# Loads of token mixtures ordered behind the copies of dense sums, one load for each copy

## The chip, the cores and the metric

One core of one Trainium2 chip runs the whole kernel. The metric is the device time of one execution in microseconds (us). The core has a matrix engine (TensorE, PE in the profile), a vector engine (VectorE, DVE), an engine for activations (ScalarE, ACT), a general engine (GpSimd, POOL), and an engine that here only issues transfers (SyncE, SP). All of them take their instructions in order, each from a queue of its own, and meet through semaphores.

## The reference

For 2048 tokens x of width 512 (float32), with 32 heads of width 16 and a hidden width of 1792:

```
g   = sigmoid(sum(x * gate_w))                         # one gate per token
q, k, v = split(x @ wqkv)                              # 32 heads of 16
a   = concat_heads(softmax(q k^T / 4) v) @ wo
b   = (sigmoid(x @ w_gate) * (x @ w_up)) @ w_down
out = g * a + (1 - g) * b
```

## The kernel before

Scores are the main work: for each of the 16 pairs of heads the kernel makes the 2048 x 2048 scores of both heads twice. Once, keys by queries, they go through the exponential into the product with the values (`st_part`, line 646, and `values`, line 787). Once before that, queries by keys, they only give each query's maximum (`sm_step`, lines 300 and 302). The maxima are transposed by VectorE into tiles `mt` (line 324), and four small transfers (line 330) put them as two extra rows into the tile `qs` that holds the queries of the pair. There are two `qs` tiles, used by alternate pairs. So `st_part` can begin on a block of 512 queries only when the maxima of this block have landed in `qs`. One block of one pair takes four steps of the main loop; in each step TensorE works on both heads of the pair, on a piece of "dense" work, and ends with the 32 matmuls of `values`.

The dense work is taken from the generator `filling` and spread over the steps, 24 half matmuls to one sum. A sum is one 128x512 tile in the PSUM bank `dn`, and takes two steps. First come 24 sums of the projections of q and k (line 154 is the matmul). After the last matmul of a sum ScalarE copies `dn` into SBUF: this is the function `leave` (line 578). GpSimd then splits the copy into a high and a low part (lines 255 and 252), and SP stores both to DRAM, to `q_d` or to `k_d` (line 254). After these 24 sums come those of the gate and up projections. They do not multiply by x itself but by "token mixtures", sums and differences of blocks of x (the table `MIX`), that the kernel makes itself while the first 24 sums run:

- `mixing(pair)` makes them in 16 pieces for one half of the tokens, one piece for each dense sum: a load of parts of x into an SBUF buffer (line 341; two buffers in turn), an addition on GpSimd (line 346), a cast and a subtraction (362, 350), and a store of 512 KB to DRAM, to `xm_d` (line 351). A load into a buffer waits until the store of the piece before last, which used it, has been written.
- `mixed(pair, j)` makes four loads from `xm_d` into one SBUF tile, `xm`, 512 KB each (line 371), and puts them on the list `parts`. The buffer is one that held x for the projections, and is free when the sums with that part of x are done.
- `take(n, behind)` issues the next n loads of this list. With `behind` it adds a dependency: the load waits for that instruction.

For the first half of the tokens the lists are filled after sums 12, 16, 22 and 24, and one load is taken after each sum up to the 20th, two after each later one. The call, inside `filling`, is

```
left = leave(e.bitcast(F32), run.o)
...
take(2 if runs > 21 else 1, left if runs < 21 else None)
```

What sets the order: on TensorE, ScalarE, VectorE and GpSimd the instructions stand in the order in which the program is written (`ORDERED`). SP is not among these; where its transfers stand is decided by the framework's scheduler, by what each one waits for. Nearly all of the kernel's transfers are issued on SP's queue, and every one of this document is. SP issues them in order, so that one that waits holds all behind it.

The functions that the change touches, and what calls them:

Of the kernel before, what the change touches and what calls it, by code (L numbers as in the profile page):

```python
# [52 lines left out]
def gated_mix(ctx, tc, x, xc, xmix, wqk, wv, wo, w_gu, w_down, gate_w, out):  # L53
# [439 lines left out]
    def filling():  # L493
# [19 lines left out]
        for j, (n, cp) in enumerate(jobs):  # L513
            settle([raw for raw, _, _ in coming])
            ws, nxt = nxt, []
            for c in range(2):
                for i, w in enumerate(ws):
                    run = Sum(bankd(), unit(w, 2 * cp + c))
                    yield run
                    runs += 1  # L520
                    e = keep.tile([P, 512], F32R, name=f"qk{n}_{cp}_{c}_{i}", tag="er", bufs=6)
                    left = leave(e.bitcast(F32), run.o)
                    put_qk(e, (q_d, k_d)[i], n, 2 * cp + c)
                    next(mix, None)
                    if j + 1 < len(jobs):
                        if (c, i) == (0, 0):
                            coming = raws(jobs[j + 1][0])
                        elif (c, i) != (1, 1):
                            nxt.append(split_weights(coming[len(nxt)]))
                    elif (c, i) != (0, 0):  # L530
                        weights()
                    if runs in (12, 16, 22, 24):
                        T[len(T)] = mixed(0, len(T))
                    take(2 if runs > 21 else 1, left if runs < 21 else None)
# [4 lines left out]
        for cp in range(2):  # L539
            for fp in range(NF // 2):  # L540
                for a in range(2):
                    arrive = combine(cp, fp, a)
                    order = [(j, g) for j in range(3) for g in ((LOW, UP) if a else (UP, LOW))] + [(3, LOW if a else UP)]
                    ws = []
                    for q, (j, g) in enumerate(order):
                        if len(ws) <= j:
                            ws.append(W.pop(0))
                        run = Side(bankd(), g, ws[j], T[j])
                        yield run
                        m = ((2, 1), (4, 3), (7, 6), (5, 5))[j][g]  # L550
                        e = keep.tile([P, 512], F32, name=f"m{m}_{cp}_{fp}_{a}", tag="er", bufs=6)
                        leave(e, run.o)
                        if arrived:
                            arrived.pop(0)()
                        arrived.append(lambda arrive=arrive, m=m, e=e: arrive(m, e))
                        if q in (0, 2, 3, 4, 6):
                            weights()
                        if t % 4 == 1:
                            next(mix, None)
                        t += 1  # L560
                        if cp == 0 and fp == NF // 2 - 1 and a == 1 and q in (2, 4, 6):
                            late_t[q // 2 - 1] = mixed(1, q // 2 - 1)
                        take(1 if late_t and q < 4 and not cp else 2)
                        if cp and fp == NF // 2 - 1 and a:
                            if q == 1:
                                load_ahead()
                            elif q > 1:
                                weights_ahead()
# [6 lines left out]
    exps, lately = [], [None]  # L575

    def leave(e, o):
        lately[0] = act.activation(e, o, AF.Copy)  # L578

    fill = filling()  # L580

# [486 lines left out]
```

## Time and profile before

| | |
|---|---|
| Time before, median of 3 runs | 1666.73 us (1665.47 to 1667.89) |
| Time of the profiled execution | 1666.75 us |
| Its span, from the first to the last instruction | 1664.9 us |
| Mean granted TensorE clock | 0.997 |
| TensorE matmuls busy | 1651.4 us, 99% of the span |
| VectorE, ScalarE, GpSimd busy | 86%, 80%, 63% |
| Transfers on SP's queue | 233.37 MB, 47.1% of 16 DMA engines |

Rows of a timeline give the start in us from the start of the span, the duration, the engine, the line of the code, the operation, what it writes and reads ("out<-in"), and how many such instructions stand together. "SPq" is SP's queue: its rows are the issues of transfers, not the transfers. In brackets stands the idle time of the engine just before, and what ended it. A row of windows gives the start and end of a stretch, its length, the busy time of each engine with the number of its instructions, the mean granted TensorE clock (1.00 is full speed), the mean busy share of the 16 DMA engines and their GB/s. A row of waits gives who waited for whom: the sum in us, how often, the longest.

### The profile page before, as it was taken

How to read it: one execution, taken by the hardware profiler on the slowest of the kernel's cores; microseconds unless marked ns; L12 is line 12 of the kernel's file. 1: busy time of each engine (PE TensorE's matmuls, PEld its weight loads, DVE VectorE, ACT ScalarE, POOL GpSimd, SP SyncE). 2: the span in 40 equal slices, each digit the busy share in tenths (PEclk: the TensorE clock that was granted, in tenths of full speed). 3: DMA queues.
4: the chain of work that ended last, by engine and by line, in shares of the span. 5: the costliest groups of instructions: out<-in, count | busy, mean ns of one | idle time of the engine just before them, and what ended most of it. 6: DMA issues, size and time to landing. Idle time of an engine off the chain costs nothing.

```text
span 1664.9 us, 44107 instructions
## 1 busy us (share of the span) xinstructions
PE 1651.4 (99%) x16842; PEld 1180.0 (71%) x16842; DVE 1427.0 (86%) x2456; ACT 1334.3 (80%) x2928; POOL 1051.8 (63%) x1238
## 2 busy tenths in 40 slices
PE   9999989999999999999999999999999999999999
PEld 7866756666666666766766766766776776678887
DVE  6989979999999999999999999999999999667643
ACT  4188868889889888888888999999999988974321
POOL 1146654457888888767666897877777767753110
PEclk9999989999999999999999999999999999999999
DMA  9624675364444434442347453424343425269850
GB/s 260 133 81 163 192 224 162 104 180 128 139 149 128 147 121 138 123 129 78 96 131 194 146 143 116 114 97 100 99 103 95 111 84 179 80 231 298 297 172 26
DMA packets 131555, 236.71 MB, mean 142 GB/s; under 512 B 19408, under 2 KB 39888, under 8 KB 128336
## 3 DMA queue, kind: packets, MB, share of 16 engines
q1 hardware_dynamic: 131056, 233.37, 47.1%
q8 instruction: 133, 2.18, 0.6%
q14 instruction: 78, 0.64, 0.2%
q10 hardware_dynamic: 288, 0.52, 0.1%
HBM read 155.71 MB, written 77.59 MB: 140 GB/s over the span
## 4 chain that ended last, share of the span: by engine, by line
PE 98%; DVE 1%; DMA 1%; POOL 0%; SPq 0%; ACT 0%; issue 0%; POOLq 0%; DVEq 0%
PE dn L174 26%; PE sm L787 17%; PE st L787 12%; PE dn L154 7%; PE sm L300 6%; PE sm L646 6%; PE sm L1004 6%; PE st L646 4%; PE st L141 4%; PE st L300 4%; PE dn L1004 2%; PE st L154 1%; PE st L1004 1%; DVE stat L302 1%; DMA xm_d<-xm 0%; PE st L89 0%
## 5 line engine op out<-in xcount | busy, mean ns | idle before, releaser
L302 DVE TENSOR_REDUCE stat<-sm 128x1 f32<-128x512 f32 x1199 | 763.2, 681 | 77.9 <-PE st L646 52.5
L648 ACT ACTIVATE p<-sm 128x512 f32<-128x512 f32 (+1 forms) x1314 | 668.4, 593 | 15.4 <-PE sm L646 14.1
L302 DVE TENSOR_REDUCE stat<-st 128x1 f32<-128x512 f32 x849 | 549.7, 681 | 46.7 <-PE sm L646 45.2
L648 ACT ACTIVATE p<-st 128x512 f32<-128x512 f32 (+2 forms) x982 | 515.6, 594 | 1.2 <-PE st L646 0.5
L174 PE MATMUL dn<-xm,mh 64*128 64x512 f32 x1568 | 484.6, 389 | 0.0
L646 PE MATMUL sm<-qs,ks 64*128 64x512 f32 (+1 forms) x1314 | 472.8, 383 | 7.8 <-DMA qs<-mt 7.8
L300 PE MATMUL sm<-ks,qs 48*128 48x512 f32 x1199 | 476.7, 420 | 0.1
L646 PE MATMUL st<-qs,ks 64*128 64x512 f32 (+2 forms) x982 | 362.9, 382 | 0.7 <-DVE v L627 0.7
L300 PE MATMUL st<-ks,qs 48*128 48x512 f32 x849 | 357.7, 422 | 0.0
L174 PE MATMUL dn<-xm,ml 64*128 64x512 f32 x784 | 303.9, 388 | 0.0
L174 PEld LDWEIGHTS dn<-xm,mh 64*128 64x128 f32 x1568 | 289.7, 185 | 14.6
L646 PEld LDWEIGHTS sm<-qs,ks 64*128 64x128 f32 x1314 | 235.1, 187 | 70.9 <-DVE stat L302 59.2
L787 PE MATMUL sm<-p,v 128*17 128x256 f32 x4672 | 280.6, 381 | 0.0
L300 PEld LDWEIGHTS sm<-ks,qs 48*128 48x128 f32 x1199 | 210.8, 184 | 33.3 <-ACT p L648 26.7
L787 PEld LDWEIGHTS sm<-p,v 128*17 128x17 f32 x4672 | 122.9, 97 | 130.3 <-ACT p L648 44.7
L646 PEld LDWEIGHTS st<-qs,ks 64*128 64x128 f32 x982 | 177.8, 187 | 48.0 <-DVE stat L302 44.9
L787 PE MATMUL st<-p,v 128*17 128x256 f32 x3520 | 211.4, 381 | 0.1
L813 POOL TENSOR_TENSOR sum<-sum,part 128x256 f32<-128x256 f32 x192 | 141.5, 737 | 66.7 <-ACT part L792 29.6
L425 POOL TENSOR_TENSOR m<-m,m 128x512 f32<-128x512 f32 x140 | 178.1, 1290 | 4.2 <-ACT m L578 2.1
L300 PEld LDWEIGHTS st<-ks,qs 48*128 48x128 f32 x849 | 157.3, 185 | 22.7 <-ACT p L648 20.1
L787 PEld LDWEIGHTS st<-p,v 128*17 128x17 f32 x3520 | 92.7, 97 | 98.2 <-ACT p L648 33.5
L174 PEld LDWEIGHTS dn<-xm,ml 64*128 64x128 f32 x784 | 144.3, 184 | 9.9
(314 smaller groups left out, 2342.8 us busy)
## 6 DMA issues: line engine op xcount, KB each, us to landing
r<-in_w_gu_dram SPq DMA_DIRECT2D x112, 256.0 KB
gul<-gu_d SPq DMA_DIRECT2D x56, 512.0 KB
gu_d<-m SPq DMA_DIRECT2D x84, 256.0 KB
xm_d<-xm SPq DMA_DIRECT2D x32, 512.0 KB
xm<-xm_d SPq DMA_DIRECT2D x32, 512.0 KB
xm<-in_xmix_dram SPq DMA_DIRECT2D x24, 512.0 KB
qs<-q_d SPq DMA_DIRECT2D x90, 128.0 KB
ks<-k_d SPq DMA_DIRECT2D x90, 128.0 KB
```

Source lines behind the costliest of these rows:

```text
L141: pe.matmul(o, a, b, start=(i == 0), stop=(i == len(ops) - 1))
L154: mm = pe.matmul(self.o, a[rows], b[rows], start=(self.n == 0), stop=(self.n == 2 * len(self.ops) - 1))
L174: pe.matmul(self.o, a, b, start=(self.n == 0), stop=(self.n == len(self.ops) - 1))
L300: pe.matmul(t, qs[r:r + KM, qt * P:(qt + 1) * P], ks[r:r + KM, g * 512:(g + 1) * 512], start=True, stop=True)
L302: dve.tensor_reduce(stat[part][:, qt % 4, g:g + 1], t, axis=AX.X, op=ALU.max)
L425: pool.tensor_tensor(o, x, y, op)
L646: pe.matmul(o, ks[r:r + KR, (kt + a) * P:(kt + a + 1) * P], qs[r:r + KR, c * 512 + lo:c * 512 + hi], start=True, stop=True)
L648: exps.append(act.activation(pt[:, a, lo:hi], o, AF.Exp, scale=DH ** -0.5))
L787: pe.matmul(o[r:r + VW, :], v[:, 4 * k % 16 + a, h * VW:(h + 1) * VW], pts[b][:, a, 256 * i:256 * i + 256], start=(a == 0), stop=(a == 3))
L813: added.append(pool.tensor_tensor(s, s, e, ALU.add))
L1004: pe.matmul(down[t], a, b, start=(f == 0 and m == 0), stop=(f == NF - 2 and m == 5))
```

## The change

The function `leave` now returns the copy that it issues. Before, it returned nothing, so that `left` in the call above was `None` in every run, and `take` added no dependency to any load.

```
     def leave(e, o):
         lately[0] = act.activation(e, o, AF.Copy)
+        return lately[0]
```

With it, each load that `take` issues after the sums 12 to 19 (eight loads, all of `xm_0` and `xm_1` for the first half of the tokens) waits for ScalarE's copy of the sum after which it is taken. The loads after sum 21 are called with `None` as before, and the other caller of `leave` does not use what it returns. Lines from 579 on have a number one higher than before.

On TensorE, VectorE, ScalarE and GpSimd every instruction stands where it stood. SP's queue is another one around these loads. The rows below are SP's; `xm_0` and `xm_1` are the two tiles loaded, `mt_i_b` are the maxima of block i for the head b of a pair, `xm_2_1` and the like are pieces of mixtures, `r_...` are weights of the gate and up projections. First, the stretch around sum 12. Before:

```order
L330 DMA qs_103<-mt_2_0_2693 2x4x32 x4
L371 DMA xm_0_2860<-xm_d 128x2x512 x3
L351 DMA xm_d<-xm_2_1_2621 256x1x512
L371 DMA xm_0_2860<-xm_d 128x2x512
L109 DMA k3r<-in_wqk_dram 128x512
L341 DMA xm_2_3_2947<-in_xmix_dram 128x1024
L391 DMA r_0_0_0_4457<-in_w_gu_dram 128x512
L391 DMA r_0_0_0_4459<-in_w_gu_dram 128x512
L371 DMA xm_1_3508<-xm_d 128x2x512
L254 DMA k_d<-qh_1_2859 128x512
```

With the change:

```order
L330 DMA qs_103<-mt_2_0_2693 2x4x32 x4
L109 DMA k3r<-in_wqk_dram 128x512
L391 DMA r_0_0_0_4457<-in_w_gu_dram 128x512
L351 DMA xm_d<-xm_2_1_2621 256x1x512
L391 DMA r_0_0_0_4459<-in_w_gu_dram 128x512
L341 DMA xm_2_3_2947<-in_xmix_dram 128x1024
L371 DMA xm_0_2860<-xm_d 128x2x512
L254 DMA k_d<-qh_1_2859 128x512
```

Five loads stood between the maxima `mt_2_0` and the store of `k_d`; one stands there now, just ahead of that store.

Second, the next maxima of head 0, those of block 3, with what each transfer waits for ("DMAHW" with a number is the semaphore of an earlier transfer, "Pool", "DVE", "Activation" and "PE" are the engines). Before:

```order
L371 DMA xm_1_3508<-xm_d 128x2x512 [waits DMAHW7_49]
L371 DMA xm_1_3508<-xm_d 128x2x512 [waits DMAHW0_49]
L371 DMA xm_1_3508<-xm_d 128x2x512 [waits DMAHW1_49]
L351 DMA xm_d<-xm_2_2_2784 256x1x512 [waits DMAHW2_49,Pool_49]
L341 DMA xm_3_0_3109<-in_xmix_dram 128x512 [waits DMAHW3_49,DMAHW2_49]
L254 DMA q_d<-qh_2_3020 128x512 [waits DMAHW4_49,Pool_49]
L254 DMA q_d<-qk_1_0_0_3018 128x512 [waits DMAHW5_49,Pool_49]
L330 DMA qs_103<-mt_3_0_3015 2x4x32 [waits DMAHW6_49,DVE_49]
```

With the change:

```order
L351 DMA xm_d<-xm_2_2_2784 256x1x512 [waits DMAHW3_49,Pool_49]
L341 DMA xm_3_0_3109<-in_xmix_dram 128x512 [waits DMAHW4_49,DMAHW3_49]
L371 DMA xm_0_2860<-xm_d 128x2x512 [waits DMAHW5_49,Activation_49]
L254 DMA q_d<-qh_2_3020 128x512 [waits DMAHW6_49,Pool_49]
L254 DMA q_d<-qk_1_0_0_3018 128x512 [waits DMAHW7_49,Pool_49]
L330 DMA qs_103<-mt_3_0_3015 2x4x32 [waits DMAHW0_49,DVE_49]
```

The three loads ahead of the store of the piece `xm_2_2` are gone from there. One load, with a wait for ScalarE, stands behind the load of the next piece, and ahead of the stores of `q_d` and the maxima.

Third, the stretch around sum 17, where two blocks later the maxima of head 0 stand behind loads of keys for the next pair. Before:

```order
L264 DMA qs_103<-q_d 16x2048
L264 DMA ks_104<-k_d 16x2048 x2
L254 DMA q_d<-qh_2_3670 128x512
L254 DMA q_d<-qk_1_0_0_3668 128x512
L264 DMA ks_104<-k_d 16x2048
L330 DMA qs_101<-mt_1_0_3665 2x4x32 x4
```

With the change:

```order
L264 DMA qs_103<-q_d 16x2048
L264 DMA ks_104<-k_d 16x2048
L371 DMA xm_1_3508<-xm_d 128x2x512
L254 DMA q_d<-qh_2_3670 128x512
L254 DMA q_d<-qk_1_0_0_3668 128x512
L264 DMA ks_104<-k_d 16x2048 x2
L330 DMA qs_101<-mt_1_0_3665 2x4x32 x4
```

Here a load and one more transfer of keys stand ahead of the maxima than before.

More of the change, by code (lines that the diff above doesn't have):

```diff
@@ L578, in leave @@
         lately[0] = act.activation(e, o, AF.Copy)
+        return lately[0]
     fill = filling()
```

## The prediction

> **What bounds the kernel now.** I read the page's busy times and its chain first, then the group of TensorE with idle time in front of it, then windows around that idle time, and last SP's queue there. From the page:
>
> ```profile
> PE 1651.4 (99%) x16842; PEld 1180.0 (71%) x16842; DVE 1427.0 (86%) x2456; ACT 1334.3 (80%) x2928; POOL 1051.8 (63%) x1238
> ...
> PE 98%; DVE 1%; DMA 1%; POOL 0%; SPq 0%; ACT 0%; issue 0%; POOLq 0%; DVEq 0%
> ...
> L646 PE MATMUL sm<-qs,ks 64*128 64x512 f32 (+1 forms) x1314 | 472.8, 383 | 7.8 <-DMA qs<-mt 7.8
> ```
>
> TensorE is 99% busy and 98% of the chain. The change removes no matmul, so what can be won is idle time of TensorE, and the time in which its clock is low. The third row has nearly all the idle time there is in the middle of the kernel: 7.8 us, and it ended when a transfer of maxima (`qs<-mt`) landed. Where, is told by the timeline of TensorE and a table of windows:
>
> ```profile
> 230.98 1.92 PE L787 MATMUL st<-p,v 128*17 128x256 f32 x32
> 236.41 1.92 PE L787 MATMUL st<-p,v 128*17 128x256 f32 x32
> 246.12 0.49 PE L646 MATMUL sm<-qs,ks 64*128 64x192 f32 x1 [7.79 <-DMA qs<-mt]
> ...
> 251.95 1.27 PE L787 MATMUL sm<-p,v 128*17 128x256 f32 x20
> ```
>
> ```profile
> core 0: us, PE busy (x) PEld busy (x) DVE busy (x) ACT busy (x) POOL busy (x), PEclk, DMA share, GB/s
> 238.30:246.10 7.80, 0.03 (x4) 0.01 (x1) 0.22 (x2) 0.38 (x1) 2.90 (x6) 0.68 0.47 160
> 246.10:251.30 5.20, 5.18 (x25) 4.47 (x27) 3.25 (x5) 3.68 (x8) 0.17 (x1) 0.50 0.63 233
> 257.40:1400.00 1142.60, 1142.60 (x12853) 793.91 (x12855) 1054.61 (x1898) 1029.52 (x2344) 847.38 (x1004) 1.00 0.43 124
> ```
>
> A step of the main loop ends with `values` (line 787). Two of them are 236.41 - 230.98 = 5.43 us apart, so the next was due at 236.41 + 5.43 = 241.84 us. It came at 251.95. **This one place costs 251.95 - 241.84 = 10.11 us**: 7.79 of idle time, and 2.32 because the first 5.2 us of work after it ran at a clock of 0.50 (second row). In the last row TensorE is busy for all of 1142.6 us at full clock: there is nothing more to win behind it.
>
> Now SP's queue, from the maxima of block 2 (208.46) to those of block 3, whose landing ended the wait; then a link of the chain there:
>
> ```profile
> 208.46 2.67 SPq L330 DMA_DIRECT2D qs<-mt  x4
> 211.23 1.91 SPq L371 DMA_DIRECT2D xm<-xm_d  x3
> 213.24 0.57 SPq L351 DMA_DIRECT2D xm_d<-xm  x1
> 213.86 0.85 SPq L371 DMA_DIRECT2D xm<-xm_d  x1
> ...
> 222.10 0.34 SPq L341 DMA_DIRECT2D xm<-in_xmix_dram  x1
> ...
> 223.48 0.52 SPq L371 DMA_DIRECT2D xm<-xm_d  x1
> ...
> 230.68 1.96 SPq L371 DMA_DIRECT2D xm<-xm_d  x3
> 232.74 0.57 SPq L351 DMA_DIRECT2D xm_d<-xm  x1
> 240.79 0.34 SPq L341 DMA_DIRECT2D xm<-in_xmix_dram  x1
> 241.22 0.38 SPq L254 DMA_DIRECT2D q_d<-qh  x1
> ...
> 242.17 2.75 SPq L330 DMA_DIRECT2D qs<-mt  x4
> ```
>
> ```profile
> 244.30 1.62 DMA qs<-mt
> ```
>
> All eight loads of `xm_0` and `xm_1` (line 371) are issued in these 24 us, in bunches of three, one, one and three. Twice a store of a piece (line 351) stands right behind three loads of 512 KB. Twice SP then stands at the next load of a piece (line 341), which needs that store written: from the issue of the store to that of the load pass 222.10 - 213.24 = 8.86 us and 240.79 - 232.74 = 8.05 us. What is behind comes late with it. GpSimd and ScalarE show when it could have gone:
>
> ```profile
> 210.31 1.27 POOL L350 TENSOR_TENSOR xm<-xm 128x512 fp32r<-128x512 f32 x1
> ...
> 216.87 1.29 POOL L252 TENSOR_TENSOR qk<-qk,qh 128x512 fp32r<-128x512 f32 x1
> ...
> 221.14 1.27 POOL L350 TENSOR_TENSOR xm<-xm 128x512 fp32r<-128x512 f32 x1
> ...
> 227.73 1.29 POOL L252 TENSOR_TENSOR qk<-qk,qh 128x512 fp32r<-128x512 f32 x1
> ```
>
> ```profile
> 226.27 0.70 ACT L578 ACTIVATE qk<-dn 128x512 f32<-128x512 f32 x1
> ```
>
> The piece stored at 232.74 was ready at 221.14 + 1.27 = 222.41. The data of `q_d` were ready at 227.73 + 1.29 = 229.02, and left after 241.22: 12.2 us late. The maxima of block 3 stand behind them. They left at 242.17 and landed at 244.30 + 1.62 = 245.92, 3.75 us after the first issue; TensorE had needed them at 238.3.
>
> **The change part by part.** It adds no instruction to an engine's work. It moves eight transfers on SP and gives each a wait for a copy by ScalarE.
>
> *The bunches go.* In the changed order a store of a piece stands behind no load of `xm` but that of the sum before. What a store needs without a bunch, from its issue to the load that waits for it, earlier rows show:
>
> ```profile
> 146.75 0.57 SPq L351 DMA_DIRECT2D xm_d<-xm  x1
> 152.11 0.33 SPq L341 DMA_DIRECT2D xm<-in_xmix_dram  x1
> ```
>
> That is 152.11 - 146.75 = 5.36 us, against 8.05 and 8.86 behind loads. I walk down the new queue with 5.36, since no more than one load is now ahead, and with 8.86 as the worst. An issue of a load of `xm` takes 1.96 / 3 = 0.65 us, that of a piece 0.34 plus some 0.1 between, two stores of q or k 242.17 - 241.22 = 0.95, the four of maxima 2.75, the store of sums (`pv_d`) as long as one of `q_d`, 0.4.
>
> With 5.36: store of piece `xm_2_1` when GpSimd has it, 210.31 + 1.27 = 211.58. Next piece issued at 216.94, load at 217.4, out by 218.0. The stores of `k_d` need GpSimd until 216.87 + 1.29 = 218.16; out by 219.1, maxima of head 1 by 221.9, sums by 222.3. The next piece is ready at 222.41 (above), the load behind it goes at 227.8, the load of `xm` at 228.2 to 228.9. `q_d` is ready at 229.02 and out by 230.0. The maxima of block 3 start at 230.0 and have landed 3.75 later, at 233.7. They are needed at 238.3: **4.6 us to spare, the wait is gone.**
>
> With 8.86 at both stores: the loads behind them go at 220.44 and, since SP comes to the second store only at 225.6, at 234.4. Then load of `xm`, `q_d` and maxima: 234.8 + 0.65 + 0.95 = 236.4, landed at 240.2. That leaves a wait of 1.9 us. In the window 238.3 to 246.1 the mean clock was 0.68; with only 1.00 and 0.50 as its values, (1 - 0.68) / 0.5 x 7.8 = 5.0 us of it were slow, so the clock fell 2.8 us after the work stopped. A wait of 1.9 us would keep the clock. I take 0 from the range 0 to 1.9, because the slow writes were those behind bunches.
>
> *The added wait.* The load in front of `q_d` waits for the copy that ends at 226.27 + 0.70 = 226.97, before SP arrives there (228.2). Right behind it stand the stores of the same copy's parts, which GpSimd makes after it, at 229.02. So whatever stands behind the load waits for later work than the load does: cost 0. Without that cover (another transfer between the two that is ready earlier) it would be the time from SP's arrival to the copy, and in the two further places that I looked at, the order has the stores right behind too.
>
> *Loads in new places.* Four of them now stand ahead of maxima of head 0, which have the least time to spare. What a load costs in the transfer engines is bounded by this answer for 200 to 260 us:
>
> ```profile
> DMA packets 6803, 13.10 MB, mean 218 GB/s; under 512 B 747, under 2 KB 1131, under 8 KB 6763
> ...
> q1 hardware_dynamic: 6795, 13.00, 67.8%
> ```
>
> 218 / 0.678 = 322 GB/s when busy, so 512 KB are 1.6 us, and 0.65 of issue: 2.3 us against 4.6 to spare. In the third place one more transfer of keys stands there. Two of those took SP 0.89 us in the pair before:
>
> ```profile
> 186.38 0.89 SPq L264 DMA_DIRECT2D ks<-k_d  x2
> ```
>
> So half of 0.89 more, 0.45: cost 0, with 4.6 - 2.3 - 0.45 = 1.9 us left even if the load's 2.3 come wholly on top. The bound above is 1.9 us of wait in each of four places, 7.6 us, if every store is slow.
>
> *Later.* The last load is issued after sum 19 instead of at 232, and the first matmuls that read these tiles come after sum 24. A sum takes 2 x 5.43 = 10.9 us, so five sums are 54 us of cover against the few us of a transfer. Cost 0.
>
> *Sum.* Against the profiled execution's own 1666.75 us (span 1664.9 and 1.85 around it): 1666.75 - 10.1 = 1656.6. The median, 1666.73, differs by 0.02 and gives the same.
>
> The Trainium skill, "TensorE: Matmul & The Clock Gate", section "Part 1: The HAM clock gate (the "warmup" mystery)", says that the clock halves after an idle window of about 3.4 us and comes back after as long a busy one. The slow 5.2 us are longer than that, and by its half speed the slow stretch would cost 5.2 x 0.5 = 2.6 us, not 2.3; the sum would be 1656.3.
>
> **The rivals.**
>
> *A rest of the wait stays.* Then only part of the 12.2 us of lateness goes. Of the eight loads ahead of `q_d` two stay; if only the issue of the other six is saved, 6 x 0.65 = 3.9 us, a wait of 7.8 - 3.9 = 3.9 us stays, long enough for the clock to fall: up to 3.9 + 2.3 = 6.2 us of the 10.1 lost, 1662.8. With one slow store it is 1657 to 1659. For it: all other transfers of this stretch stay, and the share of 67.8% is high. Against it: 4.6 us to spare by the walk.
>
> *The wait moves.* It could reappear at full size at the maxima of block 1 of the next pair, where keys and a load stand ahead of them. 10.1 us there give 1666.7: no change. For it: the order has two transfers more there. Against it: it needs the lateness of 7.8 + 4.6 = 12.4 us, and the row of the keys has 0.89.
>
> *The loads hold SP.* Each waiting load is a stop in the only queue. If stops and stores keep SP late at all four places, each maxima transfer could miss its time. From 3.4 us of loss in each place (13.4 in all: the 10.1 won and 0.2% of 1666.7, or 3.3, more) the kernel is slower; with waits of 5 us and the slow clock after each, 4 x (5 + 2.3) - 10.1 = 19 us, 1686. For it: one queue in order. Against it: the copy is done 1.2 us before SP comes (226.97 against 228.2), and even two slow stores give 1.9. The Trainium skill, "DMA: Bandwidth & Descriptors", section "Anatomy of one DMA — SWDGE (gpsimd) path", has the rule behind this rival: a wait for a semaphore is kept by the issuing sequencer before it dispatches, so a waiting transfer stops all behind it. The trace agrees in that SP stood 8.05 us at line 341 with `q_d` ready behind.
>
> *It does nothing.* The order shows the loads moved, so I give this no chance of its own.
>
> **How the numbers follow.** The wait gone: 0.80, at 1656.6. A rest: 0.09. Moved whole: 0.05. Slower: 0.06. The three runs of before lie within 1.3 us of the median, so the likeliest case spans 1655.3 to 1658.5 with the 1.9 of the slow stores. For 8 in 10 I go up into the rest's cases: 1655.0 to 1660.5. A measurement of this kernel tells about 0.2%, 3.3 us, from no change. Faster by more: 0.80 + 0.09 = 0.89; same 0.05; slower 0.06.
>
> **What would show it.** Right: no idle time before line 647 (646 now) for `qs<-mt`; steps of 5.43 us all through from 90 to 1400 us; no clock of 0.50 in the middle; on SP single loads some 10.9 us apart, line 341 at most 6 us after the store it needs, maxima of block 3 issued near 230. Wrong: a gap of more than 5.5 us between two `values` at any of the four maxima behind loads, or SP standing at line 371 with ScalarE's copy as the releaser while maxima are ready.

## The result, and the profile after

The changed kernel takes 1656.78 us (median of 6 runs, 1656.44 to 1657.49) against 1666.98 for the kernel before beside it (6 runs, 1665.47 to 1668.41): 10.2 us less, a ratio of 0.994 with a 95% interval of 0.9927 to 0.9953. The prediction was 1656.6.

The page of the changed kernel has, in the places shown before:

```profile
PE 99%; DVE 1%; ACT 0%; issue 0%; POOL 0%; DVEq 0%
...
L647 PE MATMUL sm<-qs,ks 64*128 64x512 f32 (+1 forms) x1314 | 471.3, 382 | 0.2 <-DVE mxs L314 0.2
```

The 7.8 us of idle time that ended with `qs<-mt` are gone from the group of `st_part` (now line 647), and transfers from the chain. The timeline of TensorE and the windows at the same place (line 788 is `values`):

```profile
236.28 1.92 PE L788 MATMUL st<-p,v 128*17 128x256 f32 x32
241.70 1.92 PE L788 MATMUL sm<-p,v 128*17 128x256 f32 x32
```

```profile
238.30:246.10 7.80, 7.80 (x84) 6.12 (x86) 6.97 (x14) 6.85 (x17) 6.08 (x9) 1.00 0.62 209
246.10:251.30 5.20, 5.20 (x63) 3.64 (x61) 4.92 (x10) 4.63 (x11) 2.60 (x4) 1.00 0.60 173
257.40:1390.00 1132.60, 1132.35 (x12737) 786.55 (x12735) 1045.63 (x1881) 1020.89 (x2325) 841.24 (x994) 1.00 0.43 126
```

The step that took 15.54 us before (251.95 - 236.41) takes 241.70 - 236.28 = 5.42. TensorE is busy for all of the first two windows, at full clock. In the last, 0.25 us are missing from 1132.6, in one step of 5.69 us that ends at 1001.66; the rest of the kernel runs as before. So the 10.1 us come from this one place.

SP's queue, from the maxima of block 2 to those of block 3:

```profile
208.09 2.67 SPq L330 DMA_DIRECT2D qs<-mt  x4
...
211.78 0.58 SPq L351 DMA_DIRECT2D xm_d<-xm  x1
...
215.61 0.33 SPq L341 DMA_DIRECT2D xm<-in_xmix_dram  x1
216.03 0.61 SPq L371 DMA_DIRECT2D xm<-xm_d  x1
...
222.48 0.58 SPq L351 DMA_DIRECT2D xm_d<-xm  x1
225.54 0.34 SPq L341 DMA_DIRECT2D xm<-in_xmix_dram  x1
226.86 0.60 SPq L371 DMA_DIRECT2D xm<-xm_d  x1
227.55 0.55 SPq L254 DMA_DIRECT2D q_d<-qh  x1
228.91 0.33 SPq L254 DMA_DIRECT2D q_d<-qk  x1
229.33 2.72 SPq L330 DMA_DIRECT2D qs<-mt  x4
```

There is one load for each sum, 226.86 - 216.03 = 10.83 us apart. From the store of a piece (line 351) to the load behind it (line 341) pass 3.83 and 3.06 us, where it was 8.86 and 8.05. The maxima of block 3 are issued from 229.33 and no longer from 242.17.

### The profile page after: what moved, and what is told of

The parts are those of the page before. It is cut to its first block, busy times and chain, and to the rows that moved or that the text cites. A ratio compares the mean times of both kernels' runs of the same rounds, so it can differ in the third digit from the quotient of the medians.

```text
span 1655.0 us, 44114 instructions
## 1 busy us (share of the span) xinstructions
PE 1649.0 (100%) x16842; PEld 1179.1 (71%) x16842; DVE 1430.6 (86%) x2456; ACT 1333.8 (81%) x2928; POOL 1053.2 (64%) x1238
## 4 chain that ended last, share of the span: by engine, by line
PE 99%; DVE 1%; ACT 0%; issue 0%; POOL 0%; DVEq 0%
PE dn L174 26%; PE sm L788 17%; PE st L788 13%; PE dn L154 8%; PE sm L300 6%; PE sm L647 6%; PE sm L1005 6%; PE st L647 4%; PE st L300 4%; PE st L141 4%; PE dn L1005 2%; PE st L154 1%; PE st L1005 1%; DVE stat L302 1%; PE st L89 0%; ACT p L649 0%
```

## The experiments

All variants are compared with the kernel before run beside them, whose median was 1667.05 to 1667.27 us in these comparisons. My theory was that SP is held at line 341 by stores that crawl behind bunched loads. The rivals: that it is the bytes of the loads in the transfer engines; that any bunch is enough; and that it is the wait and not the spread that helps.

That SP stood at line 341, and that the maxima were late for it, the chain of the kernel before shows by itself:

```profile
232.74 8.04 DMA xm_d<-xm
...
240.79 0.34 SPq L341
```

SP's wait ends when the store of the piece is written. From there the chain goes on over the stores of `q_d` and the issues of the maxima to the landing that TensorE waited for. SP's own wait there was 7.4 us; the 8.05 us of the prediction begin with the issue of the store. What the chain does not tell is why the store took so long, and whether something else would have made the maxima late without it.

### One buffer more for the pieces: it did not take the wait away

In the kernel before, the pieces get a third buffer, so that a load need not wait for the store just issued. The room comes from two other rings; a control has the narrower rings alone. The edit:

```
-  tag="ev", bufs=2      +  tag="ev", bufs=3         (not in the control)
-  tag="wr", bufs=6      +  tag="wr", bufs=5
-  tag="part", bufs=2    +  tag="part", bufs=1
-  warm: [P, 96]         +  warm: [P, 64]
```

> The kernel before, with all eight loads as free and as bunched as they were, but with three buffers for the mixture pieces in place of two (room for it comes from five raw-weight buffers in place of six and one buffer for the partial sums in place of two). The next load of a piece now needs the store of the piece before, not of the one just issued behind the loads. My theory (SP stands at line 341 until a store that crawls behind the loads is written, and the maxima stand behind): SP is no longer held there, the wait of 7.8 us for the maxima is gone or under 1 us, the time is 1656.5 to 1659. Rival (the bytes of eight loads in the transfer engines delay the maxima themselves): the loads are all there in the same 24 us, so the wait stays at 6 us or more and the time at 1664 to 1668.

> The control of the run with three buffers: the kernel before with five raw-weight buffers and one for the partial sums, but two buffers for the pieces. Both theories: the wait of about 7.8 us for the maxima and the slow clock after it stay, 1665 to 1669. If the narrower buffers cost something of their own, it shows here.

Measured: 1676.82 us (ratio 1.0059, 1.0042 to 1.0075), the control 1680.03 (1.0078, 1.0063 to 1.0093). I had expected 1665 to 1669 of the control. The narrower rings cost time of their own: between 90 and 1400 us nearly three quarters of the steps (171 of 237 in the variant) take 5.48 or 5.49 us in place of 5.43. The wait for the maxima stayed in both, 6.9 and 7.1 us. But the experiment did not do what I built it for. SP's order in the variant with three buffers:

```order
L371 DMA xm_1_3508<-xm_d 128x2x512 x3
L351 DMA xm_d<-xm_2_2_2784 256x1x512
L341 DMA xm_3_1_3270<-in_xmix_dram 128x512
L254 DMA q_d<-qh_2_3020 128x512
```

The scheduler has moved each load of a piece forward by one: behind the store of `xm_2_2` now stands not the load of `xm_3_0` but that of `xm_3_1`, and that is the one which takes over the buffer of `xm_2_2`. So SP stands at line 341 for the same store as before. The timeline of SP in this variant:

```profile
233.05 0.57 SPq L351 DMA_DIRECT2D xm_d<-xm  x1
241.15 0.34 SPq L341 DMA_DIRECT2D xm<-in_xmix_dram  x1
```

From the issue of the store to that of the load pass 241.15 - 233.05 = 8.10 us, nearly as in the kernel before. The run says nothing between the theory and the rival of the bytes, though my expectation spoke of it as a test.

### The loads of pieces off SP's queue: the maxima leave on time

In the kernel before, ScalarE issues the sixteen loads of line 341 of the first half. All loads of `xm` stay free, and the scheduler puts them as four, one and three (before: three, one, one and three).

```
-  sp.dma_start(f[:, :n, :], xmix[pair, j, b, :, :n, :])
+  (sp if pair else act).dma_start(f[:, :n, :], xmix[pair, j, b, :, :n, :])
```

> The kernel before, with all eight loads free, but the sixteen loads of mixture pieces for the first half of the tokens (line 341) are issued by ScalarE and no longer by SP. The bytes and the bunches stay; SP no longer stands at line 341. My theory (SP is held at line 341): the stores of q and the maxima leave on time, no wait over 1 us, 1656.5 to 1660, the loads of pieces costing ScalarE 16 issues in its idle time. Rival (the bytes of the bunches delay stores and maxima in the transfer engines): the wait stays at 5 us or more, 1663 or more.

Measured: 1663.11 us (1661.18 to 1664.55; ratio 0.9971, 0.9961 to 0.9981). No wait for maxima is left, as my theory had it; the time is that of the rival, for a reason given below. SP's timeline and GpSimd's:

```profile
227.50 2.22 SPq L371 DMA_DIRECT2D xm<-xm_d  x3
229.82 0.79 SPq L351 DMA_DIRECT2D xm_d<-xm  x1
234.54 0.33 SPq L254 DMA_DIRECT2D q_d<-qh  x1
235.91 0.33 SPq L254 DMA_DIRECT2D q_d<-qk  x1
236.33 2.74 SPq L330 DMA_DIRECT2D qs<-mt  x4
```

```profile
234.59 1.29 POOL L252 TENSOR_TENSOR qk<-qk,qh 128x512 fp32r<-128x512 f32 x1
```

Three loads and the store of a piece still stand right ahead, as in the kernel before. But nothing holds SP behind them: the data are ready at 234.59 + 1.29 = 235.88 and the store of `q_d` leaves at 235.91, where it left 12.2 us late before. So a bunch of three and a store right ahead do not make SP late when line 341 does not stand behind them. The run is not the kernel before in all else: its first bunch of loads starts at 202.52 and not at 211.23, ahead of the stores of `q_d` before, and so only one bunch is left in front of these maxima. It agrees with the chain above, but would not settle the cause alone. The gain was lost in another queue:

```profile
PE sm L300 <- ACT part L792: 3.2, 1, 3.2
```

```profile
206.97 8.64 DMA q_d<-qh
215.64 0.04 issue
215.68 0.33 ACTq L341 DMA_DIRECT2D xm<-in_xmix_dram  x1
216.06 0.38 ACT L792 ACTIVATE part<-sm 128x256 f32<-128x256 f32 x1 [4.93 <-DMA q_d<-qh]
```

ScalarE now stood at line 341, until a store of 256 KB that took 8.64 us was written, and its own work was queued behind that. This store is one of q, not the store of a piece that frees the buffer; the section on several loads behind one copy comes back to it. The steps around it are 5.62 and 0.51 us too long (11.05 and 5.94), 6.1 together, near the 6.3 between this variant and the changed kernel. The load of a piece still stands and waits, now on ScalarE and for another transfer.

### Only one of the two tiles waits

```
-  left if runs < 21 else None
+  left if runs < 16 else None                       (the first tile waits)
+  left if runs >= 16 and runs < 21 else None        (the second tile waits)
```

> Only the loads of the first tile (after sums 12 to 15) wait for copies; the four of the second tile are free, and stand two ahead of and two behind one store. My theory: one slow store of 8 to 9 us delays the maxima by about 3.5 us, inside the 4.6 us to spare, so no wait over 1 us and 1656.5 to 1658. Rival (lateness adds up with the number of free loads): half of the 12.2 us, 6.1 us late, a wait of 1.5 us, 1658 to 1660. Rival (any bunch brings the wait back): 7.8 us and 1666.

> Only the loads of the second tile (after sums 16 to 19) wait; the four of the first tile are free and stand three ahead of and one behind the store of the earlier piece. My theory: the first store is slow as before (8.9 us), the second has no bunch (5.4 us or less), so the maxima of block 3 land some 1.5 us before they are needed: no wait, 1656.5 to 1658. Rival (any bunch brings the wait back): a wait of several us, 1660 to 1666.

Measured: 1658.63 us (0.9952, 0.9937 to 0.9967) with the first tile waiting, 1657.41 (0.9944, 0.9929 to 0.9959) with the second. In the second, no wait, as I expected. In the first TensorE waited 1.53 us for the maxima, where I had expected none over 1; the figure is that of the rival by which lateness adds up. With the first tile waiting:

```profile
223.67 1.24 SPq L371 DMA_DIRECT2D xm<-xm_d  x2
225.00 0.57 SPq L351 DMA_DIRECT2D xm_d<-xm  x1
225.62 1.86 SPq L371 DMA_DIRECT2D xm<-xm_d  x2
232.29 0.34 SPq L341 DMA_DIRECT2D xm<-in_xmix_dram  x1
...
234.46 2.77 SPq L330 DMA_DIRECT2D qs<-mt  x4
```

One bunch of four makes one store slow (232.29 - 225.00 = 7.29 us) and the issue of the maxima 234.46 - 229.33 = 5.1 us later than in the changed kernel. That alone would have been in time: the last of the four was issued at 236.61, and with the 1.62 us of the kernel before it would have landed at 238.2, while TensorE came to wait at 240.71 - 1.53 = 239.18. But it took 3.96 us to land. So what my expectation had left out is that the maxima's own transfer can be slow too. With only the second tile waiting, the maxima of block 3 were issued from 233.64 and no wait came of it. With both bunches free the wait was 7.8 us. So each bunch has its part, and neither alone makes the whole.

### Waits, but several loads behind one copy

These keep the wait for a copy and change only how many loads stand behind it: four (after sums 12 and 16, ahead of stores of k; or 13 and 17, ahead of stores of q), all eight after sum 13, or two behind every second copy.

```
-  take(2 if runs > 21 else 1, left if runs < 21 else None)
+  take(2 if runs > 21 else 4, ...)                  (8 for all eight)
+  take(2 if runs > 21 else 2 - 2 * (runs % 2), ...) (two behind a k copy)
+  take(2 if runs > 21 else 2 * (runs % 2), ...)     (two behind a q copy)
   the lists are filled after sums 13 and 17 where the copies are of q,
   both after sum 13 for all eight
```

> With waits, but four loads behind one copy: those of the first tile behind the copy after sum 12, those of the second behind the copy after sum 16, both just ahead of stores of k and of the maxima of head 1, that have more time. My theory: no store of a piece stands close behind the bunch, so no wait over 1 us, 1656.5 to 1658.5. Rival (one load for each copy is what counts, any bunch of four costs): a wait of 2 to 8 us, 1659 to 1667.

> As the run with four loads behind one copy, but after sums 13 and 17, so that the bunch stands just ahead of the stores of q and of the maxima of head 0, that have the least time. My theory: four issues of 0.65 us and some 2.7 MB at 322 GB/s (8.4 us from 227.3) bring the landing of the maxima to 234 (issue alone) to 236.5 (behind the bytes), before 238.3: no wait over 1 us, 1656.5 to 1658.5. Rival (a bunch is what costs): a wait of 2 us or more, 1659 to 1667.

> All eight loads behind the copy after sum 13, just ahead of the stores of q and of the maxima of block 3 of head 0. If the maxima do not queue behind the bytes: eight issues of 0.65 us, landing at about 236.5, no wait, 1657. If they do: 4.9 MB at 322 GB/s from 227.3 are 15 us, landing at about 242, a wait of 3 to 4 us, with the slow clock up to 6 us lost, 1660 to 1663. My theory of the kernel before needs neither, but it says that what counts is the lateness of the maxima and not the number of loads.

> With waits, two loads behind every second copy (after sums 12, 14, 16 and 18), just ahead of the stores of k and of the maxima of head 1. By the earlier runs one load in each place costs nothing and four cost about 3.4 us. Theory (a threshold: lateness costs nothing until the time to spare is used up, each load adding about 0.65 of issue and 1.6 of transfer): no wait over 0.5 us, 1656.4 to 1658. Rival (the cost grows with each load beyond the first): about 1.1 us, 1658 to 1659.

> With waits, two loads behind the copies after sums 13, 15, 17 and 19, just ahead of the stores of q and of the maxima of head 0. Theory (threshold): with one load the maxima of block 3 were issued from 229.3 and had landed by some 233.4; one load more adds 2.3 us, 235.7, before 238.2: no wait over 0.5 us, 1656.4 to 1658. Rival (grows with each load beyond the first): a third of the 3.4 us of the run with four, 1658 to 1659.

| loads behind one copy | us | ratio (95% interval) | longest idle time of TensorE that it caused |
|---|---|---|---|
| 1 (the change) | 1656.78 | 0.994 (0.9927 to 0.9953) | none |
| 2, copies of q | 1656.81 | 0.9939 (0.9922 to 0.9955) | none |
| 2, copies of k | 1657.50 | 0.9942 (0.9927 to 0.9957) | 0.46 us |
| 4, copies of q | 1660.88 | 0.9964 (0.995 to 0.9978) | 1.92 us |
| 4, copies of k | 1661.35 | 0.9967 (0.9956 to 0.9979) | 1.71 us |
| 8, a copy of q | 1666.47 | 0.9994 (0.9984 to 1.0003) | 7.1 us |

My theory failed for four loads: I had expected no wait in either place. It held for two. With all eight behind one copy the whole gain is gone, though each load waits as in the change. What SP and the transfers did there:

```profile
227.50 6.54 SPq L371 DMA_DIRECT2D xm<-xm_d  x8
234.14 1.11 SPq L254 DMA_DIRECT2D q_d<-qh  x1
235.34 0.80 SPq L254 DMA_DIRECT2D q_d<-qk  x1
236.25 6.74 SPq L330 DMA_DIRECT2D qs<-mt  x4
```

```profile
SPq L330 <- DMA xm<-xm_d: 4.1, 3, 2.1
```

```profile
231.38 10.98 DMA xm<-xm_d
242.36 0.02 issue
242.38 3.23 DMA qs<-mt
```

Here it isn't line 341 that holds SP behind the bunch: the bunch stands behind that line. The issue of four maxima takes 6.74 us and not 2.7, because SP waits three times for loads of `xm` to land; the last that counted needed 10.98 us, and the maxima landed at 242.38 + 3.23 = 245.6. I had put the landing at 242 for this case.

So the rival of the bytes is no rival but a second way to the same wait, and it has two parts. With eight loads the larger one is again SP standing. The load of 10.98 us is the sixth of the eight, and the maxima transfer that it released is the last of four, eight places behind it. With four loads ahead of stores of q the second load (7.90 us) released the last of the maxima, again eight places behind, and the store of q that ScalarE stood for above is eight transfers ahead of its load. The rows of the change show where this comes from: each transfer waits for one of the semaphores DMAHW0 to DMAHW7, which follow in turn from row to row, so that a transfer is not issued before the one eight places ahead of it has landed. No run here changes the number eight.

The other part is in the maxima's own transfers: the last one took 3.23 us here, where it took 1.62 us in the kernel before. With four loads ahead of stores of q it took 4.55 us, from 235.82, and this part alone made the wait: with 1.62 it would have landed at 237.4, and TensorE came to wait at 238.58. TensorE waited at both bunches there, 1.92 and 1.26 us.

With four loads ahead of stores of k a third way shows, one that I had not thought of. The chain of that run at the second bunch:

```profile
263.25 7.60 DMA k_d<-qh
...
272.00 5.90 DMA xm<-in_xmix_dram
...
277.95 0.61 POOL xm L362
```

```profile
PE dn L154 <- POOLq L194: 1.7, 1, 1.7
```

The store of k took 7.60 us, GpSimd's cast stood until it was written, then GpSimd's work on a piece stood 5.1 us until the piece had landed. In GpSimd's queue behind it is the token with which a dense sum passes to its second half (`turn`, line 194), and TensorE waited for this token. The 0.46 us with two loads ahead of stores of k ended with the same token.

### The wait met early: the spread is what counts

Each load waits for the copy of the sum before its own, the first for none:

```
-  take(2 if runs > 21 else 1, left if runs < 21 else None)
+  take(2 if runs > 21 else 1, before if runs < 21 else None)
+  before = left
```

> As the changed kernel, one load for each sum, but each load waits for the copy of the sum before (the load after sum 12 for none), so that the wait is met long before SP comes. Six of the loads stay in the same places in the queue, one (the first) stands right behind the maxima of block 2 and ahead of a store of a piece. Theory (what counts is that the loads are spread, not that they wait): no wait over 0.5 us, 1656.4 to 1658, and SP not waiting for ScalarE at line 371. Rival (the wait itself must hold the load until the copy): the loads move up and bunch again, a wait of 1.5 us or more, 1658 or more.

Measured: 1656.95 us (0.9939, 0.9924 to 0.9954), the same as the change, and no wait of TensorE for maxima. SP's waits at the loads, first in this variant and then in the changed kernel, both from 205 to 300 us:

```profile
SPq L371 <- ACT p L650: 3.1, 6, 0.6
SPq L371 <- ACT qk L579: 0.6, 1, 0.6
```

```profile
SPq L371 <- ACT qk L578: 13.1, 7, 2.9
```

In the change SP stands 13.1 us in all for the copies; in the variant the profile puts 0.6 down to a copy and 3.1 to other work of ScalarE, 3.7 in all and never more than 0.6 at once, so the wait is met early though not always before SP comes. The time is the same. So standing there neither helps nor costs; the dependency matters because the scheduler then spreads the loads over the sums. That SP would not wait for ScalarE at all, as I had expected, did not come true.

## Why the prediction was right, step by step

- *One place costs 10.11 us, and the change removes it whole:* right. 10.2 us by the medians, and the step there is 5.42 us.
- *The walk down the new queue:* the maxima of block 3 were to be issued from 230.0; they were issued from 229.33. The walk took 5.36 us from a store to the load behind it; it was 3.83 and 3.06. (The kernel before has rows of 3.02 and 3.03 us as well, for the stores at 125.02 and 135.86.) That the walk came out within 0.7 us all the same is no proof of this term: in the walk and in the run the stores of `q_d` wait for GpSimd, whose part was ready at 229.02 by the walk and was stored from 228.91.
- *What holds SP is the load at line 341 behind a crawling store:* shown for the kernel before by its chain, and borne out by the variant with the loads on ScalarE's queue. That the store crawls because of the bunch is argued from the stores: 8.05 and 8.86 us with both bunches free, 9.28 and 7.29 where only the first or only the second was, 3.06 and 3.83 in the change. As a general account of why bunches cost it was too narrow: with eight loads behind one copy SP stands for the loads themselves, with four the maxima land late, with four ahead of k GpSimd is late. The prediction counted a load in a new place at 2.3 us and four places apart; for one load that was enough.
- *The added wait costs 0:* the number is right, the first reason is wrong. I had SP at the load in front of `q_d` at 228.2, after the copy; the stores of pieces were faster, and SP came earlier and stood 0.9 us, until the copy ended at 226.83. The second reason, that what stands behind needs later work on the same copy, is what held: the time is that of the variant in which the wait is met early.
- *A wait under 2.8 us keeps the clock* (in the bound of the slow stores): wrong, below. The sum did not rest on it, but the range did, and too low: a wait of 1.92 us cost 3.41.
- *The rivals:* no rest of the wait stayed, and it did not move to the maxima of the next pair, although a load and more keys stand ahead of them; the loads did not hold SP long enough to matter.

## What to carry to other kernels

When a queue is ordered by a scheduler, a transfer that waits for no late work can be moved forward into a bunch; a dependency on work that comes once for each transfer spread them here, and it was not the wait itself that helped. Look for what stands behind a bunch in the same queue and needs its transfers written: the wait that the profile shows on the compute engine can be several transfers away from its cause. And before counting a bunch as harmless, walk every queue that it delays, not only the one that has the least time to spare.

## What was not expected of the hardware

The clock of TensorE fell after shorter idle times than the 2.8 us worked out from the kernel before. These are windows around the waits with four loads behind copies of q, with four behind copies of k, and with only the first tile waiting, in this order:

```profile
238.60:245.50 6.90, 5.00 (x29) 3.91 (x29) 3.80 (x8) 4.39 (x10) 2.99 (x6) 0.75 0.59 192
```

```profile
274.80:283.70 8.90, 7.20 (x66) 4.70 (x65) 5.20 (x9) 5.42 (x12) 3.56 (x6) 0.81 0.67 188
```

```profile
238.00:245.00 7.00, 5.47 (x69) 3.73 (x65) 5.12 (x11) 4.96 (x12) 4.23 (x7) 1.00 0.50 165
```

Idle times of 1.92 and 1.71 us brought a slow stretch, those of 1.53 and 1.26 us none. With 1.00 and 0.50 as the only values, the first two slow stretches are (1 - 0.75) / 0.5 x 6.9 = 3.5 us and (1 - 0.81) / 0.5 x 8.9 = 3.4 us long. Each step there lost 3.4 us in all (8.84 and 8.87 in place of 5.43), so the clock nearly doubled the price of the wait. Nor is the fall a time after the work has stopped, as the 2.8 us took it to be: in the first run TensorE works again from 240.50, the clock is still 1.00 from 240.60 to 241.40, and it is 0.50 from 241.60 to 244.80. The Trainium skill, "TensorE: Matmul & The Clock Gate", section "Part 1: The HAM clock gate (the "warmup" mystery)", puts the window at about 3.4 us, free-running, which agrees with the length of the stretches. The Trainium skill's table there has the clock fall only after a whole idle window; here it fell after 1.92 and after 1.71 us with TensorE busy before and behind, so that rule does not hold for this kernel. Where between 1.53 and 1.71 us the line lies, and whether it depends on when the idle time begins, stays open.
